# A hand-written step plan laid out anew: hedgehog linear attention plus a Mish layer on one Trainium2 core

## The chip, the cores and the metric

The kernel runs on one core of a Trainium2 chip. The metric is device time in microseconds: the median of 3 runs of the kernel before is 175.88 us (175.77 to 176.64). Engines are named as in the profile: PE is TensorE's matmul, PEld its weight loads, DVE is VectorE, ACT is ScalarE, POOL is GpSimd, SP is SyncE, which here only issues DMAs. A "q" behind an engine (SPq, ACTq) is its instruction queue.

## What is computed

The input x has 2048 rows of 512 bf16 numbers. Each row is normalised, and the result goes through two branches whose outputs are added to x.

```python
xn = _layernorm(x)                                   # 2048 x 512
qkv = xn @ wqkv                                      # 32 heads of 16
pq, pk = q @ w_phi, k @ w_phi                        # per head, 16 x 16
phi_q = concat(softmax(pq), softmax(-pq))            # 32 features a head
phi_k = concat(softmax(pk), softmax(-pk))
kv, z = phi_k^T @ v, sum of phi_k                    # over all 2048 rows
o = (phi_q @ kv) / (phi_q . z + 1e-6)
out = x + o @ wo + mish(xn @ w1 + b1) @ w2           # w1: 512 x 1792, w2: 1792 x 512
```

## The kernel before

The rows are cut into 16 tiles of 128 (numbered 0 to 15) and into four groups of four tiles. Nothing in the kernel loops: a text called `PLAN` (line 20) lists 582 steps by name, and the loop at line 710 carries them out one after the other with `step` (line 595). The order of the names is the order in which instructions stand in each engine's queue, since the tile framework's scheduler is switched off (line 158). Each engine works through its own queue in order; semaphores keep the data dependences. A last number in the names `apply`, `sums` and all that end in `=` picks the engine: 0 is ACT and 1 DVE for the steps that end in `=`; for `apply`, `sums` 0 is DVE, 1 POOL, 2 ACT.

The steps, in the order in which the work needs them:

- Normalising: `spread`, `mean` or `gather` (DVE statistics of a tile), `total` and `scatter` (the same on ACT for tile 3), `deviate` (ACT square root), `invert` (DVE reciprocal), `apply` (writes the normalised tile). Tiles 0 to 3 are then turned on PE (`flip`, line 255, four transposes into a PSUM bank) and copied to SBUF (`flip=`); tiles 4 to 15 are turned by DMA on SP's queue (`turned`, line 263).
- Weights: `foldk` multiplies the key weights with w_phi on PE (line 172, four small matmuls a step, four steps), `foldk=` casts the result into `wkv` on ACT; `fold` and `fold=` do it later for the queries. The two halves of the turned key weights `wT` come by DMA (line 167).
- Attention, keys: `first_i_kt` (tile i of the first group, a quarter of its contraction, line 632) and `logits_g_i` (four matmuls, line 662) give pk; `logits=` copies it out of PSUM, `plane` subtracts the extremes (DVE), `exp` is the exponential on ACT, `sums` and `normal` finish the softmax, `value` and `value=` give v, and `add` (line 445) adds a tile to kv on PE.
- Attention, queries: the same with s = 4 to 7 (`logits`, `logits=`, `minus=`, `shift`, `exp`, `sums`, `weigh`), then `kv` (masks kv on DVE), `turn` (DMA transpose on SP, line 418), `attend` (eight matmuls on PE into a single buffer `pnd`, line 484), `divide` (DVE), `out` (DMA transpose on SP, line 512).
- Dense branch: `unit_g_f` (four matmuls, line 288) and `unit=` (Mish on ACT, line 300), 56 of each.
- End of a tile: `second_t_0`, `second_t_1` (seven matmuls each, line 520), `project_t` (four matmuls, line 530), `residual_t` (DVE adds x, line 539), `store_t` (DMA to HBM on SP's queue, line 544; tile 15 is stored in two halves, one of them from ACT's queue).

Exponentials and Mish need different tables on ACT, so every change from `exp` to `unit=` or back costs a table load. Six PSUM banks go round in a ring (`bank`, line 130): a step on PE that opens a bank waits until the step that empties the bank opened six before it has run. `warm` is a matmul of ones that nobody reads (line 582): eleven run at the start (line 588), two more stand in the plan.

Of the kernel before, what the change touches and what calls it, by code (L numbers as in the profile page):

```python
# [26 lines left out]
logits=_0_3_1 root_1 logits=_0_2_1 first_1_3 value=_1_0 value_2 logits=_0_1_1 unit_0_6 bias=  # L27
apply_6_0 unit_0_2 apply_7_0 unit=_0_6 plane_0_0 turned_6 apply_4_2 value_0 apply_5_2 unit_0_11
value=_0_0 turned_4 unit_0_12 value=_2_0 unit=_0_2 unit_0_4 spread_11 unit=_0_12 spread_12 unit_0_3
unit=_0_11 plane_0_1 unit=_0_4 unit_0_10 unit=_0_3 value_3 w2 unit=_0_10 logits_1_2 spread_9  # L30
logits_1_3 exp_0_1 value=_3_1 value_4 spread_13 logits=_1_3_0 sums_0_1_1 spread_10 logits_1_1
exp_0_0 spread_8 value_7 value=_4_0 gather_2 logits=_1_1_0 logits=_1_2_1 unit_0_0 exp_0_3 spread_14
logits_1_0 root_2 spread_15 exp_0_2 unit_0_8 sums_0_0_0 value=_7_0 unit_1_13 gather_3 apply_8_0
unit_1_9 apply_11_0 apply_9_0 unit=_0_0 apply_10_0 unit_0_1 logits=_1_0_1 unit=_1_9 root_3 turned_10
unit_1_3 sums_0_2_0 unit=_0_8 unit=_1_13 turned_8 unit_1_11 normal_0_0 unit=_0_1 unit_1_6 apply_12_2
apply_15_2 value_6 unit=_1_3 unit_0_5 apply_14_0 wo unit=_1_11 plane_1_0 add_0_0 unit=_1_6 unit_1_12
turned_14 value=_6_0 unit_1_5 apply_13_2 unit_1_2 unit=_1_12 turned_12 unit=_0_5 sums_0_3_0 unit_1_7
unit=_1_2 unit_1_1 plane_1_1 unit=_1_7 unit=_1_5 logits_2_3 unit=_1_1 value_5 logits=_2_3_0
logits_2_0 normal_0_1 logits_3_3 exp_1_3 add_0_1 logits_2_1 exp_1_0 logits_2_2 sums_1_3_0 value=_5_0
sums_1_0_1 exp_1_1 unit_2_3 logits=_2_0_1 add_0_2 logits=_2_1_0 sums_1_1_0 add_0_3 logits_3_2  # L40
logits=_3_3_0 exp_1_2 unit_2_2 normal_1_0 masks logits=_2_2_0 unit_2_1 logits_3_0 unit=_2_3 unit_1_8
sums_1_2_0 logits=_3_2_0 wq unit_1_0 unit=_2_2 unit=_2_1 plane_2_0 unit_3_1 unit=_1_0 unit_1_4
logits=_3_0_0 unit=_1_8 unit_2_9 unit=_3_1 unit_3_12 normal_1_1 add_1_1 unit=_3_12 unit_3_9
unit=_2_9 logits_3_1 unit=_1_4 plane_2_1 add_1_0 logits=_3_1_0 unit_1_10 unit=_3_9 add_1_3
unit=_1_10 fold_1 fold_2 add_1_2 fold=_1_0 unit_2_11 fold=_2_0 fold_0 plane_3_0 unit=_2_11 unit_3_13
fold=_0_0 unit_2_8 unit=_3_13 value_14 unit=_2_8 value_9 plane_3_1 value_13 exp_2_2 value_8
value=_9_0 value_11 value=_14_0 exp_2_3 value=_13_1 sums_2_2_1 value_12 value=_8_1 exp_2_1 value_15
value=_11_1 value=_12_1 exp_2_0 fold_3 value_10 value=_15_1 exp_3_2 sums_2_1_1 sums_2_3_0 unit_0_13
exp_3_3 unit_2_5 fold=_3_1 value=_10_1 unit_3_10 exp_3_0 normal_2_1 unit_0_7 exp_3_1 unit_3_11
unit_3_8 sums_2_0_0 sums_3_1_1 unit=_0_13 add_2_3 add_2_2 unit=_2_5 unit_3_2 normal_2_0 unit=_3_10  # L50
unit_3_5 unit=_3_11 unit=_0_7 logits_4_2 unit=_3_2 unit_3_7 unit=_3_8 sums_3_0_0 sums_3_3_1
logits_4_3 unit=_3_7 unit=_3_5 add_2_0 sums_3_2_0 add_2_1 unit_2_4 logits=_4_2_0 normal_3_0
logits_4_0 minus=_4_2_0 logits=_4_3_0 logits_4_1 logits=_4_0_0 minus=_4_3_0 unit_2_0 logits=_4_1_0
shift_4_1 unit_2_13 unit=_2_4 minus=_4_0_0 unit_0_9 unit=_2_13 minus=_4_1_0 unit_3_3 unit=_2_0
unit_3_4 unit=_3_3 shift_4_0 unit=_0_9 unit_2_6 unit=_3_4 add_3_1 logits_5_1 unit=_2_6 logits_5_3
# [4 lines left out]
turn_0_1 unit=_3_6 logits_6_0 minus=_5_2_0 logits=_6_1_0 logits_7_1 turn_0_0 kv unit=_2_12  # L60
logits_7_0 logits=_6_3_0 turn_1_0 shift_5_0 minus=_6_1_0 logits_7_3 minus=_6_3_0 logits=_6_0_0
second_0_0 turn_1_1 second_2_0 shift_5_1 exp_5_0 exp_5_1 second_0_1 minus=_6_0_0 logits=_7_1_0
attend_0_0 second_1_0 sums_5_1_1 minus=_7_1_0 divide_0_0 logits=_7_3_0 logits=_7_0_0 sums_5_0_0
out_0_0 attend_0_1 minus=_7_3_0 second_2_1 minus=_7_0_0 divide_0_1 exp_5_2 second_3_0 weigh_2
second_1_1 shift_6_0 turn_2_0 out_0_1 logits_7_2 attend_1_0 second_4_0 turn_2_1 divide_1_0 exp_6_0
sums_5_2_0 project_0 exp_6_1 out_1_0 sums_6_0_1 attend_1_1 logits=_7_2_0 residual_0 second_3_1
exp_5_3 divide_1_1 minus=_7_2_0 project_1 out_1_1 shift_6_1 second_5_0 store_0 attend_2_0 second_5_1
divide_2_0 exp_6_3 project_2 sums_6_1_0 exp_6_2 out_2_0 sums_6_3_1 attend_2_1 second_4_1 divide_2_1
residual_2 out_2_1 project_3 residual_1 sums_6_2_1 second_6_0 residual_3 store_2 sums_5_3_0
second_7_0 weigh_3 second_8_0 weigh_4 turn_3_0 project_4 turn_3_1 shift_7_0 second_7_1 turn_4_0  # L70
second_10_0 turn_4_1 weigh_5 exp_7_1 project_5 store_3 exp_7_0 attend_3_0 second_10_1 divide_3_0
sums_7_0_1 residual_4 out_3_0 attend_3_1 second_6_1 divide_3_1 turn_5_0 sums_7_1_0 attend_4_0
second_8_1 turn_5_1 divide_4_0 second_12_0 weigh_6 out_3_1 out_4_0 project_6 residual_5 shift_7_1
attend_4_1 turn_6_0 second_12_1 store_1 second_9_0 divide_4_1 exp_7_3 project_7 residual_6 exp_7_2
out_4_1 sums_7_3_1 attend_5_0 second_9_1 divide_5_0 residual_7 out_5_0 attend_5_1 project_8
divide_5_1 turn_6_1 second_13_0 sums_7_2_0 store_5 second_11_0 weigh_7 out_5_1 project_9 turn_7_0
attend_6_0 second_11_1 divide_6_0 turn_7_1 attend_6_1 out_6_0 project_10 divide_6_1 second_13_1
store_4 residual_8 residual_10 store_8 project_11 out_6_1 attend_7_0 second_14_0 divide_7_0
residual_11 out_7_0 attend_7_1 project_12 divide_7_1 second_15_0 residual_12 out_7_1 residual_9
# [6 lines left out]
def kernel(  # L86
# [43 lines left out]
    def bank(name, dtype=FP32):  # L130
        return ps.tile([P, 512], dtype, name=name, tag="mm")
# [22 lines left out]
    block = consts.tile([P, 8, 16], BF16, name="block")  # L154
# [423 lines left out]
    dve, act = nc.vector.tensor_copy, nc.scalar.copy  # L578

    warm = bank("warm")  # L580

    def keep_warm():
        nc.tensor.matmul(  # L583
            warm[:].rearrange("p (k c) -> p k c", k=4), lhsT=ones[:],
            rhs=ones[:, None, :].to_broadcast([P, 4, P]), start=True, stop=True,
        )

    for _ in range(11):
        keep_warm()

    kvp = ExitStack()
# [150 lines left out]
```

## Time and profile before

| | |
|---|---|
| median of 3 runs | 175.88 us |
| the profiled execution, whole time | 175.89 us |
| its span, first to last instruction | 174.1 us |
| PE busy | 169.0 us, 1040 matmuls |
| DVE busy | 151.9 us, 268 instructions |
| ACT busy | 112.0 us, 167 instructions |
| POOL busy | 49.1 us, 91 instructions |
| read from HBM, written | 6.84 MB, 2.10 MB |

The span and the whole time differ by 1.8 us that lie around the program. In the profile a line such as L290 is a line of the kernel; "128x512" is partitions by elements. A timeline or chain row begins with the start in microseconds from the span's start, then its length. A row of a chain of waits merges neighbouring pieces of the same kind. A busy time of a matmul contains the filling of the pipeline: one of 512 columns is booked with 379 ns, while four in a row take 0.86 us, as the chain shows.

### The profile page before, as it was taken

What the parts mean: (1) busy time and instruction counts of PE and PEld (TensorE: products, weight loads), DVE (VectorE), ACT (ScalarE), POOL (GpSimd) and SP (SyncE); (2) the same over time, 40 slices, a digit from 0 to 9 for tenths busy, and PEclk for the clock granted to TensorE, in tenths of its full rate; (3) what the DMA queues carried; (4) which work ended last, traced back from release to release, by engine and by line L of the source; (5) the groups of instructions that cost most, each with busy time, mean ns of one, the idle gap of its engine ahead of it and who ended that gap; (6) DMA issues with size and microseconds to landing.
All of it is one profiled execution on the core that took longest, in us unless ns stands there. A gap on an engine that the chain in (4) does not pass through costs nothing.

```text
span 174.1 us, 2834 instructions
## 1 busy us (share of the span) xinstructions
PE 169.0 (97%) x1040; PEld 83.3 (48%) x1040; DVE 151.9 (87%) x268; ACT 112.0 (64%) x167; POOL 49.1 (28%) x91
## 2 busy tenths in 40 slices
PE   7999999999999999999999999999999999999991
PEld 2644444444544644455445444445544544545660
DVE  2999999999899999999899997999999999966722
ACT  4938999999997999998989999535400402100000
POOL 6021048100660008594008204115560410500000
PEclk9999999999999999999999999999999999999999
DMA  5999992878000000000000191163226677376571
GB/s 152 270 365 378 112 336 84 133 187 168 0 0 0 4 0 0 2 0 4 0 0 0 32 184 30 30 145 73 57 60 138 144 169 124 63 177 162 68 230 62
DMA packets 45226, 18.03 MB, mean 104 GB/s; under 512 B 37148, under 2 KB 45212, under 8 KB 45212
## 3 DMA queue, kind: packets, MB, share of 16 engines
q1 hardware_dynamic: 44524, 17.26, 43.2%
q10 hardware_dynamic: 688, 0.59, 1.1%
q8 instruction: 8, 0.13, 0.3%
q14 instruction: 6, 0.05, 0.1%
HBM read 6.84 MB, written 2.10 MB: 51 GB/s over the span
## 4 chain that ended last, share of the span: by engine, by line
PE 88%; ACT 4%; DVE 4%; issue 1%; DVEq 0%; ACTq 0%
PE po L525 28%; PE ph L290 23%; PE pproj L275 21%; PE po L534 7%; PE warm L583 3%; PE pnd L489 2%; ACT e L378 2%; PE pkv L452 2%; DVE m L341 2%; DVE e L348 1%; PE pfold L175 1%; ACT L378 1%; PE ptr L258 1%; DVE x_sb L542 1%; ACT acts L300 0%
## 5 line engine op out<-in xcount | busy, mean ns | idle before, releaser
L290 PE MATMUL ph<-xnT,w_sb 128*128 128x512 bf16 x224 | 51.8, 379 | 0.2 <-ACT acts L300 0.2
L525 PE MATMUL po<-w_sb,acts 128*128 128x512 bf16 (+1 forms) x238 | 51.8, 366 | 0.0
L378 ACT ACTIVATE e<-e 128x1024 bf16<-128x1024 bf16 x28 | 28.1, 1053 | 27.7 <-DVE e L348 27.7
L392 POOL TENSOR_TENSOR t<-e 128x512 f32<-128x512 bf16 x13 | 16.9, 1300 | 78.8 <-ACT e L378 78.8
L300 ACT ACTIVATE acts<-ph,b1f 128x512 bf16<-128x512 f32 x56 | 35.2, 702 | 1.6 <-PE ph L290 1.6
L290 PEld LDWEIGHTS <-w_sb 128*128 128x128 bf16 x224 | 21.5, 98 | 25.2 <-issue 0.5
L525 PEld LDWEIGHTS <-acts 128*128 128x128 bf16 x238 | 22.4, 98 | 22.3
L275 PE MATMUL pproj<-wkv,xnT 128*128 128x512 bf16 x128 | 29.8, 379 | 0.0
L275 PEld LDWEIGHTS <-xnT 128*128 128x128 bf16 x192 | 18.3, 98 | 21.2 <-issue 0.2
L388 DVE TENSOR_REDUCE sums<-e 128x64 f32<-128x1024 bf16 x15 | 18.0, 1210 | 0.6 <-ACT e L378 0.6
L392 POOL TENSOR_TENSOR t<-t 128x256 f32<-128x256 f32 (+1 forms) x28 | 15.8, 565 | 2.2
L534 PE MATMUL po<-wqk,ob 128*128 128x512 bf16 (+1 forms) x68 | 16.3, 366 | 0.0
L275 PE MATMUL pproj<-wqk,xnT 128*128 128x512 bf16 x64 | 15.1, 379 | 0.0
L542 DVE TENSOR_TENSOR x_sb<-po,x_sb 128x512 bf16<-128x512 f32 (+1 forms) x17 | 10.7, 652 | 4.3 <-PE po L534 4.2
L198 DVE BATCH_NORM_STATS2 stats<-x_sb 128x6 f32<-128x512 bf16 x15 | 9.7, 682 | 2.4 <-DMA x_sb<-in_A_x_dram 2.3
L505 DVE TENSOR_TENSOR ob<-pnd,r 128x512 bf16<-128x512 f32 x16 | 11.1, 692 | 0.6
L439 DVE TENSOR_TENSOR e<-e,r 128x2048 bf16<-128x2048 bf16 x8 | 9.8, 1228 | 0.3
L504 DVE RECIPROCAL r<-pnd 128x32 f32<-128x32 f32 x16 | 5.7, 354 | 4.7 <-PE pnd L489 4.4
L534 PEld LDWEIGHTS <-ob 128*128 128x128 bf16 x68 | 6.4, 98 | 6.5
L489 PEld LDWEIGHTS <-qT 128*128 128x128 bf16 x128 | 6.2, 97 | 3.8 <-issue 1.5
L434 DVE RECIPROCAL r<-sums 128x128 bf16<-128x128 f32 x8 | 7.6, 946 | 0.4 <-POOL sums L392 0.3
L348 DVE TENSOR_TENSOR e<-e,m 128x2048 bf16<-128x2048 bf16 x6 | 7.4, 1225 | 0.3
(81 smaller groups left out, 185.7 us busy)
## 6 DMA issues: line engine op xcount, KB each, us to landing
out_dram<-x_sb SPq DMA_DIRECT2D x15, 128.0 KB, 1.8
w_sb<-in_B_w_dram SPq DMA_DIRECT2D x2, 896.0 KB, 7.9
x_sb<-in_A_x_dram SPq DMA_DIRECT2D x3, 512.0 KB, 9.8
w_sb<-in_B_w_dram SPq DMA_DIRECT2D x2, 640.0 KB, 6.3
wkv<-in_A_wqkv_dram SPq DMA_DIRECT2D x1, 512.0 KB, 4.9
w_sb<-in_B_w_dram SPq DMA_DIRECT2D x1, 512.0 KB, 7.0
wqk<-in_A_wo_dram SPq DMA_DIRECT2D x1, 512.0 KB, 4.6
x_sb<-in_A_x_dram ACTq DMA_DIRECT2D x1, 384.0 KB, 3.3
```

The source lines that it names most:

```text
L198: nc.vector.bn_stats(statistics(t)[0][:, t % TPG, :], x_sb[:, t, :])
L275: nc.tensor.matmul(pp, lhsT=xnT[:, t, kt, :], rhs=w[:, kt, :], start=(kt == 0), stop=(kt == KT - 1),)
L290: nc.tensor.matmul(ph[:], lhsT=w1_sb[:, kt, f * P : (f + 1) * P], rhs=xnT[:, g * TPG : (g + 1) * TPG, kt, :], start=(kt == 0), stop=(kt == ...
L300: nc.scalar.activation(acts[:, f, g * 512 : (g + 1) * 512], ph[:], ACT.Mish, bias=b1f[:, f : f + 1])
L378: nc.scalar.activation(v, v, ACT.Exp)
L388: nc.vector.reduce_sum(out, part, axis=AX.X)
L392: nc.gpsimd.tensor_tensor(out=to[:], in0=part[:, :, 0:n], in1=part[:, :, n : 2 * n], op=ALU.add)
L439: nc.vector.tensor_tensor(out=vv, in0=vv, in1=r2[:, :, None, :].to_broadcast([P, 128, 8, 2]), op=ALU.mult)
L505: nc.vector.tensor_tensor(out=o_t.rearrange("p (u v g d) -> p u v g d", u=2, v=4, g=4), in0=nd[:, :, :, 0:64].rearrange("p u v (g d) -> p ...
L525: nc.tensor.matmul(po[:, c], lhsT=acts[:, f, t * P : (t + 1) * P], rhs=w2_sb[:, f, c], start=(f == 0), stop=False,)
L534: nc.tensor.matmul(po[:, c], lhsT=oT_of[h][:, 2 + t % 2, j * P : (j + 1) * P], rhs=wo_sb[:, j, c], start=False, stop=(j == 3),)
L542: nc.vector.tensor_tensor(out=y, in0=po[:, c], in1=y, op=ALU.add)
```

## The change

The plan is replaced as a whole. It has 581 steps instead of 582: the same ones, except for one `warm` fewer and for some steps that change engine. One matmul of ones fewer also runs ahead of the plan, 10 instead of 11. All matmuls that are used are the same in number and size.

- First tiles: tile 0 is turned before any `foldk`, and tiles 0, 2, 3, 1 are normalised and turned in that order (before: 0, then 3 and 1, then 2). The first `first` steps stand between the last turns.
- Engines: `logits=` 23 on ACT and 9 on DVE become 26 and 6, `value=` 9 and 7 become 8 and 8, `sums` 18 on DVE and 14 on POOL become 17 and 15, `apply` 11 on DVE and 5 on ACT become 12 and 4, of the first turns' copies tile 0 moves from ACT to DVE and tile 1 from DVE to ACT.
- Stores: each `store` follows its `residual` by a few steps. Before the last `out` there are 11 stores on SP's queue instead of 7. Every store is issued in the order 1, 0, 2, 3, 4, ... 15.
- The end from `project_14` on (six steps) is the same in both.

```diff
 PLAN = """
-spread_0 block mean_0 deviate_0_1 invert_0_1 total_3 spread_1 foldk_0 apply_0_0 scatter_3 foldk_1
-mean_1 flip_0 warm warm spread_2 deviate_1_1 deviate_3_1 invert_1_1 foldk=_1_0 mean_2 invert_3_1 apply_3_0
-deviate_2_1 apply_1_0 foldk=_0_0 flip_3 foldk_2 invert_2_1 apply_2_0 foldk_3 flip=_0_0 flip_1
-flip=_3_1 flip_2 foldk=_2_0 first_0_0 flip=_1_1 first_3_0 foldk=_3_0 flip=_2_1 first_0_1 first_3_1
-spread_5 first_1_0 bias first_2_0 spread_7 first_1_1 first_2_1 first_0_2 spread_4 first_3_2
-first_2_2 first_1_2 spread_6 first_0_3 first_3_3 logits=_0_0_0 first_2_3 gather_1 value_1
...
-normal_3_1 logits_5_0 exp_4_1 unit_2_7 exp_4_0 unit_3_0 logits=_5_1_1 sums_4_1_1 exp_4_2
-logits=_5_0_1 unit_2_10 minus=_5_1_0 logits=_5_3_1 add_3_0 exp_4_3 add_3_3 minus=_5_3_1 add_3_2
-logits_6_2 minus=_5_0_1 sums_4_2_1 unit_3_6 sums_4_0_0 unit=_2_7 logits_5_2 sums_4_3_0 unit=_3_0
-unit_2_12 unit=_2_10 weigh_0 logits=_6_2_0 logits_6_1 logits=_5_2_0 logits_6_3 minus=_6_2_0 weigh_1
...
-second_14_1 store_6 store_7 store_10 project_13 store_12 store_9 second_15_1 residual_13 store_13
-store_11 project_14 project_15 residual_14 store_14 residual_15 store_15
+spread_0 block mean_0 deviate_0_1 invert_0_1 total_3 spread_2 apply_0_0 scatter_3 mean_2 flip_0
+spread_1 foldk_1 deviate_2_1 foldk_0 warm flip=_0_1 deviate_3_1 foldk=_0_0 invert_2_1 foldk_2 invert_3_1
+apply_2_0 foldk_3 foldk=_1_0 mean_1 flip_2 apply_3_0 first_0_0 deviate_1_1 flip=_2_1 flip_3
+foldk=_2_0 first_0_1 invert_1_1 first_2_0 apply_1_0 foldk=_3_0 first_0_2 flip=_3_1 first_2_1 flip_1
+first_3_0 flip=_1_0 first_0_3 spread_6 first_3_1 first_2_2 logits=_0_0_0 spread_7 first_1_0
+first_3_2 first_1_1 spread_5 first_2_3 bias value_1 logits=_0_2_0 spread_4 bias= first_1_2 gather_1
+value=_1_0 first_3_3 first_1_3 root_1 logits=_0_3_1 value_2 logits=_0_1_0 unit_0_6 value=_2_1
...
+minus=_4_2_0 logits_4_0 unit=_3_8 unit_3_11 logits=_4_0_0 shift_4_1 unit=_3_5 unit_3_4 minus=_4_0_0
+unit_0_9 unit=_3_4 unit=_3_11 unit_0_7 unit=_0_9 shift_4_0 logits_5_3 unit=_0_7 add_3_2 add_3_0
+logits_5_0 exp_4_2 add_3_1 logits_5_2 logits=_5_3_1 exp_4_3 sums_4_2_1 logits_5_1 logits=_5_0_1
+exp_4_1 minus=_5_3_1 unit_3_0 minus=_5_0_1 exp_4_0 unit_2_10 logits=_5_1_1 add_3_3 logits=_5_2_0
+sums_4_1_1 sums_4_0_0 unit_2_12 minus=_5_1_0 minus=_5_2_0 unit_2_7 kv logits_6_0 sums_4_3_0
+logits_6_1 unit=_3_0 unit=_2_10 weigh_0 logits_6_2 unit=_2_12 logits_6_3 logits=_6_0_0 unit=_2_7
...
+residual_4 sums_7_1_1 turn_5_0 divide_3_1 second_8_1 store_4 residual_5 attend_4_0 store_5
+second_10_1 divide_4_0 out_3_1 sums_7_0_1 attend_4_1 turn_5_1 project_6 divide_4_1 second_12_0
+out_4_0 residual_6 shift_7_1 second_9_0 store_6 out_4_1 attend_5_0 project_7 weigh_6 exp_7_2
...
+project_12 second_15_0 store_11 residual_12 store_12 project_13 second_15_1 residual_13 store_13
+project_14 project_15 residual_14 store_14 residual_15 store_15
 """
...
-    for _ in range(11):
+    for _ in range(10):
         keep_warm()
```

More of the change, by code (lines that the diff above doesn't have):

```diff
@@ L26 @@
-first_2_2 first_1_2 spread_6 first_0_3 first_3_3 logits=_0_0_0 first_2_3 gather_1 value_1
[L27 to L54, printed above, removed]
@@ L61 @@
[L61 to L78, printed above, removed]
@@ new lines @@
+unit=_0_10 unit_0_11 unit=_0_3 value_3 unit=_0_11 w2 value_6 spread_10 logits_1_2 exp_0_2 spread_11
+logits_1_3 spread_8 exp_0_0 spread_15 logits_1_0 value=_3_0 gather_2 logits_1_1 spread_14 root_2
+logits=_1_2_0 value=_6_1 exp_0_1 value_5 spread_13 exp_0_3 unit_1_7 logits=_1_1_1 apply_11_0
+unit_1_2 logits=_1_3_0 apply_10_0 value=_5_0 apply_8_0 unit_0_1 apply_9_0 logits=_1_0_0 spread_12
+sums_0_1_1 turned_8 unit_0_5 sums_0_3_0 unit_1_3 turned_10 unit=_0_1 gather_3 sums_0_0_0 unit=_1_7
+unit_1_13 unit=_1_2 root_3 unit_0_8 sums_0_2_0 unit=_0_5 unit_0_0 unit=_1_13 normal_0_0 unit=_0_8
@@ new lines @@
+unit_1_12 unit=_1_3 unit_1_6 unit=_0_0 unit=_1_12 unit_1_9 wo apply_13_0 apply_15_2 plane_1_0
+unit_2_8 unit=_1_6 unit_1_11 apply_12_2 unit=_2_8 turned_12 value_4 unit=_1_11 unit_1_1 value=_4_0
+apply_14_0 plane_1_1 turned_14 unit=_1_9 logits_2_1 unit=_1_1 value_7 logits=_2_1_0 logits_2_0
+logits_2_3 normal_0_1 exp_1_3 logits_2_2 value=_7_0 add_0_0 exp_1_0 unit_2_11 sums_1_3_0
+logits=_2_0_0 sums_1_0_1 unit_1_4 exp_1_2 logits=_2_3_1 logits_3_2 exp_1_1 sums_1_2_0 unit_2_1
+logits=_2_2_0 sums_1_1_0 add_0_2 unit_1_5 masks add_0_1 normal_1_1 logits_3_3 unit=_2_11 unit=_1_4
@@ new lines @@
+add_0_3 unit_1_0 logits=_3_2_0 unit=_2_1 unit_3_12 wq unit=_1_5 normal_1_0 add_1_2 unit=_1_0 add_1_3
+logits_3_0 unit=_3_12 logits=_3_3_0 unit_3_9 logits=_3_0_0 plane_2_0 logits_3_1 unit=_3_9 unit_2_9
+unit_1_10 unit=_2_9 logits=_3_1_0 unit_2_3 plane_2_1 unit=_1_10 unit_1_8 unit=_2_3 add_1_0 unit=_1_8
+add_1_1 fold_0 fold_2 fold=_0_0 fold_1 unit_3_13 fold=_2_0 plane_3_0 fold=_1_0 unit_2_2 unit=_3_13
+unit_3_1 unit=_2_2 value_9 unit=_3_1 value_14 plane_3_1 fold_3 value_13 exp_2_1 value_10 value=_9_0
```

29 lines of the change are left out of this document (26 added, 3 removed).

## The prediction

> **What bounds the kernel now.** I read the page first (busy times), then the chain of waits in order of time, then the waits of PE, then the timelines of ACT and SP where the chain leaves PE. Below stand one line of the page, rows of the chain (start, length), one row of PE's timeline (13.81), one of its waits (us, times, longest), and further rows of the chain.
>
> ```profile
> PE 169.0 (97%) x1040; PEld 83.3 (48%) x1040; DVE 151.9 (87%) x268; ACT 112.0 (64%) x167; POOL 49.1 (28%) x91
> 1.12 4.88 PE warm L583 x11
> 6.00 0.58 PE pfold L175 x8
> 6.57 0.22 PE ptr L258 x4
> 6.80 0.43 PE warm L583 x2
> 7.23 0.36 PE ptr L258 x4
> 7.58 0.45 PE pfold L175 x8
> 8.03 0.46 PE ptr L258 x8
> 8.49 1.17 PE pproj L275 x5
> 9.66 0.11 PE pb L635
> 9.77 4.21 PE pproj L275 x19
> 13.81 1.89 PE L290 MATMUL ph<-xnT,w_sb 128*128 128x512 bf16 x8
> ...
> PE ph L290 <- ACT acts L300: 0.2, 1, 0.2
> ...
> 107.72 0.25 PE pnd L489 x8
> ...
> 169.49 1.02 DVE x_sb L542 x2
> 170.51 0.33 DVEq L737
> ```
>
> PE sets the time. A matmul of 512 columns takes 0.215 us (0.43 / 2), from 9.77 on PE's rows follow each other at about that (4.21 / 19), and the list of its waits has one entry behind the start, of 0.2 us. So work taken off DVE, ACT, POOL or SP is worth nothing by itself; the kernel gains only where PE starts its useful work earlier, where that one wait goes, or behind PE's end. It loses wherever a new wait stands in front of a matmul. The matmuls that are used stay the same, so there is little to gain: what lies between the ones and 9.77, the one wait, and the 4.6 us from 169.49, where DVE follows PE, to the end of the span at 174.1.
>
> **1. The start.** Useful PE work begins at 6.00 by the chain. From there to 9.77 lie 16 `foldk`, 16 turns, 5 `first` and the turn of b1. At full rate that is 32 x 0.056 (0.45 / 8) + 5 x 0.215 + 0.11 = 3.0 us; the rows take 3.77. The 0.8 us between are the two ones in the plan (0.43), slower first matmuls, and short waits. What the new order can start, and when, comes from DVE and ACT:
>
> ```profile
> 5.16 0.40 DVE L250 TENSOR_SCALAR xn<-x_sb,mv,rstd 128x512 bf16<-128x512 bf16 x1
> 6.72 0.73 DVE L250 TENSOR_SCALAR xn<-x_sb,mv,rstd 128x512 bf16<-128x512 bf16 x2
> 7.95 1.10 DVE L625 COPY xnT<-ptr 128x512 bf16<-128x512 bf16 x3
> 6.02 0.47 ACT L219 ACTIVATE rstd<-mv,eps 128x1 f32<-128x1 f32 x2
> 8.23 1.09 ACT L629 CAST wkv<-pfold 128x512 bf16<-128x512 f32 x2
> L558 SPq DMA_DIRECT2D w_sb<-in_B_w_dram x2: 496/502/507, 6.0 to 6.5; - x2
> DMA to landing us min/median/max: 7.0/7.9/8.8
> ```
>
> Ten ones at 0.44 each (4.88 / 11) end near 5.5. The turn of tile 0 needs its `apply`, which ends at 5.56 (5.16 + 0.40) and does not move: PE idles 0.1 to 0.2 us. Turn 5.6 to 6.0, eight `foldk` to 6.5, one `warm` to 6.7, eight `foldk` to 7.2. DVE copies tile 0 from 6.3 to 6.6 (0.36 each, 1.10 / 3), the square roots of tiles 2 and 3 are done at 6.5 (6.02 + 0.47), two reciprocals and `apply_2` follow the copy (in before 0.23 us lay between the square roots and 6.72, and 0.37 is one `apply`) and end near 7.3, so the second turn is at 7.4 and `first_0_0` at 7.6, against 8.49 in the chain. From there ACT's casts of `wkv` gate: from 6.7 on, one each 0.5 us (1.09 / 2), with a square root between them, the third done at 8.5 and the fourth at 9.0. Taking the `first` steps as their casts and copies come ready, `first_0_3` ends at 9.6, seven `first` and all turns done. Nine more `first` (1.94), the turn of b1 (0.11), `value_1` and `value_2` (1.73) put `unit_0_6` at 13.4. In before it began at 13.81. Gain 0.4 us. Bounds: it cannot begin before its half of w1 has landed, 6.0 + 7.0 = 13.05, which caps the gain at 0.75; if the casts or the copies each slip by one 0.36 us copy, nothing is left, so 0 is the other bound. I take 0.4, the result of the walk.
>
> The eleventh matmul of ones is worth nothing by itself: it stood before `apply_0` was ready. The one in the plan is worth its 0.215 (0.43 / 2) and is within the 0.4.
>
> **2. The wait at 96.95.** `unit_2_12` waits for `unit=_2_7`, which empties its bank six openings back.
>
> ```profile
> 89.23 1.28 ACT L378 ACT_TABLE_LOAD   x1 [0.56 <-DVE e L348]
> 90.53 2.95 ACT L378 ACTIVATE e<-e 128x1024 bf16<-128x1024 bf16 x3
> 93.38 0.58 ACT L329 ACTIVATE wkv<-pproj 128x512 bf16<-128x512 f32 x1
> 93.86 1.04 ACT L378 ACTIVATE e<-e 128x1024 bf16<-128x1024 bf16 x1
> 94.92 1.28 ACT L300 ACT_TABLE_LOAD   x1
> 96.22 1.84 ACT L300 ACTIVATE acts<-ph,b1f 128x512 bf16<-128x512 f32 x3
> 95.73 1.03 PE L275 MATMUL pproj<-wqk,xnT 128*128 128x512 bf16 x4
> 96.95 1.02 PE L290 MATMUL ph<-xnT,w_sb 128*128 128x512 bf16 x4 [0.20 <-ACT acts L300]
> ```
>
> The four matmuls from 95.73 fill 0.86, so PE stood from 96.59 to 96.95: 0.36 us. ACT was late because it idled 0.56 for DVE's `shift` and then ran table, four `exp`, a copy, table. In the new plan `exp_4_2` and `exp_4_3` come first, whose `shift_4_1` stands before `shift_4_0`. Counted from the start of `unit_0_7`, with 0.86 for four matmuls and 0.25, as the eight of an `attend`, for an `add`: its `unit=` ends at 1.7, table to 3.0, four `exp` at 0.96 to 6.8, three copies at 0.5 to 8.3, table to 9.6, `unit=_3_0` to 10.2. PE comes to `logits_6_0`, which needs the last of the three copies, at 8.8, and to `logits_6_2`, which needs `unit=_3_0`, at 10.5. Margins 0.5 and 0.3: the wait goes, worth 0.36, with bounds 0 and 0.36.
>
> The plan has other such blocks (`exp_0`, `exp_1`); the same count leaves 0.2 us at `unit_0_5` and 0.35 at `unit_1_0`. Thin, but PE stood only once in 160 us of a plan of the same kind. For new short waits I take 0.1, with bounds 0 and 1.1 (three blocks at 0.36).
>
> **3. The stores.** The first row is the nine stores at the end of SP's queue, the second the last two of them alone; the page's rows give KB and us from issue to landing.
>
> ```profile
> 165.20 6.00 SPq L546 DMA_DIRECT2D out_dram<-x_sb  x9
> 170.21 0.99 SPq L546 DMA_DIRECT2D out_dram<-x_sb  x2
> L546 SPq DMA_DIRECT2D out_dram<-x_sb x16: 332/446/585, 120.8 to 170.9; - x16
> out_dram<-x_sb SPq DMA_DIRECT2D x15, 128.0 KB, 1.8
> out_dram<-x_sb SPq DMA_DIRECT2D x1, 64.0 KB, 2.4
> ```
>
> The seven that wait there need at most 7 x 0.585 = 4.1 us from 165.20, to 169.3, and `store_14` is issued at 170.21 because `residual_14` ends there. The queue is free before the last tile is ready, so issuing them earlier moves the end by 0. What follows PE's end is the same six steps: two adds on DVE, the last half's issue, its landing, the program's close. Bounds: 0 to -0.6, if the last half lands in the 1.8 of the others instead of 2.4.
>
> What the stores cost lies earlier: four more of them stand ahead of transposes on SP's queue, 4 x 0.585 = 2.3 us of issue over 60. A transpose `out` for `project` lands by this row:
>
> ```profile
> L513 SPq DMA_TRANSPOSE ob<-ob x16: 1189/1197/1875, 109.1 to 163.4; - x16
> DMA to landing us min/median/max: 2.4/2.5/4.3
> ```
>
> The shortest way from an `out` to its `project` in the new plan, counted in matmuls on PE, is `out_3_1`: two `attend` (0.25 each), `project_6` (0.86) and two `second` (7 x 0.215 each), 4.4 us. 2.5 to land and 1.2 for the two stores right ahead make 3.7. Cost 0, with up to 1.1 if it lands in 4.3 (4.3 + 1.2 - 4.4).
>
> **4. Steps that change engine.** DVE gives up three copies and one `sums`, and takes one `value=` and one `apply`; ACT and POOL move by less than 3 us. DVE is 87% busy and PE hides it, so 0; where it would come out, at `divide` between two `attend`, the plan has fewer pairs with a single `second` between them than before (3 against 6).
>
> Sum against the profiled execution's 175.89: -0.4 - 0.36 + 0.1 + 0 + 0 = 175.2. The median of the runs, 175.88, is the same to 0.01, so nothing is added.
>
> **The rivals.** *All margins hold and the start reaches its cap*: -0.75 - 0.36, 174.8; if only the start and the wait come out and no new wait, 175.1. For it: PE waited once in 160 us in a plan of the same kind. Against it: casts of `wkv` on ACT, in order, are what gates 7.6 to 9.0.
>
> *The gain is given back in new short waits*: three blocks at 0.36 plus the 0.1, about 175.9 to 176.2. For it: margins of 0.2 to 0.35.
>
> *SP's queue* (slower). A store waits for its `residual`, and every transpose behind it waits too: `store_4` and `store_5` ahead of `out_3_1`, and likewise at `out_4_1`, `out_5_1`, `out_6_1`, `out_7_1`. At the longest landing each costs 1.1 as above; it decides from the point where a store's residual ends less than 3.7 us before the `project` that the `out` behind it feeds. Two such give 175.2 + 2.2 = 177.4. Against it: transposes land in 2.5 at the median, and most stores stand 1.5 us of matmuls or more behind their `residual`.
>
> *The clock* (slower). The chain shows 11 ones in 4.88 us, 0.44 each, and two later ones in 0.43: PE ran at half rate up to some place in the first eight `foldk` (0.58 against 0.45), near 6.1, after 5.0 us without a gap. Now it idles up to 0.2 us at 5.5, and then come transposes. If the 5.0 us began again, half rate would last from 6.1 to 10.6, 4.5 us; at half rate that does 2.25 us of work instead of 3.9 (4.5 less some 0.6 of waits in the walk), a loss of 1.7, which gives 176.9. [...]
>
> **How the numbers follow.** The forecast, 175.0 to 175.6, has 0.45; the rival with no new wait and a better start (under 175.0) 0.30; short waits (to 176.3) 0.10; SP's queue 0.09; the clock 0.06. 0.5% is 0.88 us, about what a measurement of this kernel can tell from no change: faster is under 175.00, slower over 176.76. So faster 0.30, same 0.45 + 0.10 = 0.55, slower 0.15. The range 174.7 to 176.9 holds the first three, reaches to the clock's 176.9 and leaves out two stalls of the queue; the likeliest's own is 175.0 to 175.6.
>
> **What would show it.** Right: `unit_0_6` near 13.4; no wait of PE for `acts` near 96; the chain on PE from 9.6 to 169; the last store issued as long behind PE's end as now (0.75 to 1.4 us). Wrong: ones or `foldk` at half rate behind 6.5 us; PE waiting for `ob` or `qT` behind SP; several waits on `acts`; an earlier end behind the last `project`.

## The result and the profile after

The kernel after takes 174.57 us (median of 6 runs, 174.39 to 175.06), the kernel before beside it 176.33 us (6 runs, 175.77 to 176.83): a ratio of 0.990, 95% interval 0.988 to 0.993. Every ratio below is likewise the time over that of the kernel before, run beside it. Run once more later, unchanged (the run a_again below), it took 174.96 us against 176.16: 0.993 (0.992 to 0.994). So the change gains 1.2 to 1.8 us, where 0.7 was forecast against the profiled execution.

The profiled execution after takes 174.82 us, its span is 173.1 us, against 175.89 and 174.1. Three lines of its page: the span, the busy times, and the share of each engine in the chain that ended last.

```profile
span 173.1 us, 2832 instructions
PE 167.2 (97%) x1021; PEld 82.8 (48%) x1038; DVE 151.1 (87%) x266; ACT 113.1 (65%) x168; POOL 51.0 (29%) x95
PE 72%; DVE 18%; DMA 3%; SPq 3%; issue 3%; DVEq 0%
```

PE's work is as before (some matmul records are missing: the page has 1021 of them). But 18% of the chain now runs over DVE; before it was 4%:

```profile
PE 88%; ACT 4%; DVE 4%; issue 1%; DVEq 0%; ACTq 0%
```

The waits of PE after (us in all, times, longest), and rows of the chain in order of time (start, length):

```profile
PE warm L582 <- DVE ones L563: 1.1, 1, 1.1
PE ptr L258 <- DVE xn L250: 0.4, 1, 0.4
PE pproj L275 <- DMA wkv<-in_A_wqkv_dram: 0.4, 1, 0.4
...
5.55 5.80 DMA wkv<-in_A_wqkv_dram
11.35 0.05 issue
11.40 2.56 PE pproj L275 x11
13.96 0.02 issue
13.98 0.03 DVE vext L282
...
46.50 0.61 DVE p L310
47.11 0.04 issue
47.16 1.02 PE ph L290 x4
...
95.26 1.73 PE ph L290 x8
96.99 4.10 PE pproj L275 x19
...
169.34 1.02 DVE x_sb L542 x2
170.36 0.33 DVEq L736
```

Three things are to be seen. First, the wait for `acts` near 97 is gone: at 96.99 PE goes straight from one step to the next. Second, two new waits have come: the value weights land at 11.35 and PE stands for 0.4 us in front of `value_1`, and from 13.98 to 47.11 the chain runs on DVE, which ends in a copy for which `unit_2_1` waits. That wait is not in the list of waits, and shows in PE's timeline:

```profile
45.98 1.03 PE L275 MATMUL pproj<-wkv,xnT 128*128 128x512 bf16 x4
47.16 1.02 PE L290 MATMUL ph<-xnT,w_sb 128*128 128x512 bf16 x4
```

Four matmuls from 45.98 fill 0.86, to 46.84; the next start at 47.16, 0.32 later. Third, PE ends only 0.15 us earlier: `residual_14`, the row of L542, starts at 169.34 instead of 169.49. The whole is 1.07 us shorter (175.89 less 174.82), so some 0.9 lie behind PE's end. Rows of the view of the DMAs between 170.5 and 174 us show them: the packets of each queue (count, MB, share of 16 engines) and then the two halves of the last store, with KB and us to landing. By their bytes q1 carries SP's DMAs and q10 ACT's; q14 is marked as carrying instructions. Before:

```profile
q1 hardware_dynamic: 288, 0.20, 17.3%
q10 hardware_dynamic: 144, 0.07, 6.4%
q14 instruction: 1, 0.01, 1.1%
out_dram<-x_sb ACTq DMA_DIRECT2D x1, 64.0 KB
out_dram<-x_sb SPq DMA_DIRECT2D x1, 64.0 KB, 2.4
```

And after:

```profile
q1 hardware_dynamic: 288, 0.20, 17.4%
q10 hardware_dynamic: 144, 0.07, 6.5%
out_dram<-x_sb ACTq DMA_DIRECT2D x1, 64.0 KB
out_dram<-x_sb SPq DMA_DIRECT2D x1, 64.0 KB, 1.5
```

The last half of the last tile lands in 1.55 us instead of 2.44, 0.89 less, and the one other difference in the window is a packet of the instruction queue q14. The trace has its time: it is 8 KB, starts at 171.92 us and takes 628 ns, to 172.55. In before all packets of the last store but nine start by 172.06; eight packets of 512 bytes and the closing one of 4 bytes start from 172.54 on, the moment that the instruction packet is through. So it looks as if they waited for it; the trace does not name a packet's DMA engine, so where they waited is not shown. In after the packets of the last store are all started by 171.91, and the nearest packet of q14 is at 147.72.

### The profile page after: what moved, and what is told of

The parts are those of the page before. It is cut to its first block, busy times and chain, and to the rows that moved or that the text cites. A ratio compares the mean times of both kernels' runs of the same rounds, so it can differ in the third digit from the quotient of the medians.

```text
span 173.1 us, 2832 instructions
## 1 busy us (share of the span) xinstructions
PE 167.2 (97%) x1021; PEld 82.8 (48%) x1038; DVE 151.1 (87%) x266; ACT 113.1 (65%) x168; POOL 51.0 (29%) x95
## 4 chain that ended last, share of the span: by engine, by line
PE 72%; DVE 18%; DMA 3%; SPq 3%; issue 3%; DVEq 0%
PE po L525 28%; PE ph L290 17%; PE pproj L275 15%; PE po L534 7%; DMA wkv<-in_A_wqkv_dram 3%; DVE m L361 3%; DVE e L369 3%; DVE stats L198 3%; DVE xn L250 2%; PE pnd L489 2%; PE pkv L452 2%; DVE sums L388 2%; SPq L167 2%; DVE r L434 1%; DVE e L439 1%
## 5 line engine op out<-in xcount | busy, mean ns | idle before, releaser
L392 POOL TENSOR_TENSOR t<-e 128x512 f32<-128x512 bf16 x14 | 18.5, 1324 | 65.0 <-ACT e L378 65.0
L392 POOL TENSOR_TENSOR t<-t 128x256 f32<-128x256 f32 (+1 forms) x30 | 16.9, 563 | 2.4
L388 DVE TENSOR_REDUCE sums<-e 128x64 f32<-128x1024 bf16 x14 | 16.7, 1208 | 0.7 <-ACT e L378 0.7
L542 DVE TENSOR_TENSOR x_sb<-po,x_sb 128x512 bf16<-128x512 f32 (+1 forms) x17 | 10.9, 654 | 5.9 <-PE po L534 5.8
L534 PE MATMUL po<-wqk,ob 128*128 128x512 bf16 (+1 forms) x65 | 15.6, 366 | 0.2
L327 ACT CAST e<-pproj 128x512 bf16<-128x512 f32 x12 | 6.9, 602 | 2.7 <-PE pproj L275 1.3
L310 ACT CAST p<-pproj 128x512 bf16<-128x512 f32 x13 | 7.6, 595 | 0.7 <-PE pproj L275 0.7
```

The lines of the kernel that those rows point to most:

```text
L388: nc.vector.reduce_sum(out, part, axis=AX.X)
L392: nc.gpsimd.tensor_tensor(out=to[:], in0=part[:, :, 0:n], in1=part[:, :, n : 2 * n], op=ALU.add)
L534: nc.tensor.matmul(po[:, c], lhsT=oT_of[h][:, 2 + t % 2, j * P : (j + 1) * P], rhs=wo_sb[:, j, c], start=False, stop=(j == 3),)
L542: nc.vector.tensor_tensor(out=y, in0=po[:, c], in1=y, op=ALU.add)
```

## The experiments

Theory A, the author's supposition from these rows: the packet of q14 brings ACT's next instructions (the theory's "fetch"), and its place follows how many instructions ACT has got through. In before it then comes just behind ACT's part of the last store (issued at 170.54, the packet at 171.92) and in front of the last half's packets. After has three more ACT instructions (192 ahead of ACT's last store instead of 189, waits and DMA issues counted), so it would come earlier, at 147.72. Rival B: it is the early stores that empty the queue or the DMA engines. For the 0.15 at PE's end the question was what took back the rest of the 0.4 and 0.36.

Four kernels first. **b_act3**: before, with three small instructions on ACT.

```diff
-exp_7_3 project_7 residual_6 exp_7_2 out_4_1
+exp_7_3 project_7 residual_6 exp_7_2 idle idle idle out_4_1
...
+        elif kind == "idle":
+            nc.scalar.activation(root[:], eps[:], ACT.Exp)
```

> The kernel before with three added activations of 128x1 on ACT right behind its last exponential, results unused. Theory A (instruction fetch): in the trace of before an 8 KB packet of the instruction queue q14 begins at 171.9 us, between the last half-store's issue (170.9) and its landing (2.4 us, where the changed kernel's took 1.55); ACT crosses into a new block of its instructions there, and three instructions more bring that crossing to about 148 us, as in the changed kernel. Expected: no q14 packet behind 165 us, last half-store lands in 1.5 to 1.7 us, time 0.6 to 0.9 us shorter than before. Theory B (the early stores clear the DMA queue for the last one): nothing about the stores is changed, so the landing stays at 2.4 and the time within 0.2 us.

175.26 us (174.87 to 175.53), ratio 0.9948 (0.9932 to 0.9963). More work, 0.91 us less time. The same window of its trace:

```profile
q1 hardware_dynamic: 288, 0.20, 17.3%
q10 hardware_dynamic: 144, 0.07, 6.5%
out_dram<-x_sb ACTq DMA_DIRECT2D x1, 64.0 KB
out_dram<-x_sb SPq DMA_DIRECT2D x1, 64.0 KB, 1.5
```

The packet is gone from the end, and the landing is that of after. But it did not come to about 148 us, as expected: the last two packets of q14 are at 136.58 and 150.62 (in before at 150.73 and 171.92), and the trace does not say which engine a packet is for. The wait of 0.36 near 97 is still there, and PE's work from `unit_0_6` to the last issue is as long as in before (157.05 us against 157.06).

**b_stores**: before, with every store moved close behind its `residual`, in after's manner.

```diff
-second_14_1 store_6 store_7 store_10 project_13 store_12 store_9 second_15_1 residual_13 store_13
+second_14_1 store_9 project_13 second_15_1 residual_13
...
+attend_3_1 store_4
+attend_4_1 store_5
+out_4_1 store_6
+attend_5_1 store_7
```

> The kernel before with every store moved up to two steps behind its residual, nothing else changed. Theory A: ACT's queue is as before, so the q14 packet still meets the last half-store: time within 0.2 us of before, unless transposes behind the stores come late (up to 1 us slower). Theory B: the last half-store lands in 1.5 to 1.7 us and the time is 0.6 to 0.9 us shorter.

176.08 us (175.78 to 176.64), ratio 0.9995 (0.9983 to 1.0008). The packet is there and the landing is long:

```profile
q14 instruction: 1, 0.01, 1.5%
out_dram<-x_sb SPq DMA_DIRECT2D x1, 64.0 KB, 2.7
```

**a_late**: after, with the stores of tiles 6, 7, 9, 10, 11 and 12 held back to the end.

```diff
-residual_12 store_12 project_13
+residual_12 store_6 store_7 store_10 project_13 store_12 store_9
-residual_13 store_13
+residual_13 store_13 store_11
...
```

> The changed kernel with stores 6, 7, 9, 10, 11 and 12 held back to the end of SP's queue, where before had its seven. Theory A: the time stays that of the changed kernel, 1.5 to 1.9 us shorter than before (174.5), last landing 1.5 to 1.7 us. Theory B: the last half-store lands in about 2.4 us and 0.7 to 0.9 us of the gain is lost (175.3).

175.05 us (174.51 to 175.26), ratio 0.9927 (0.9909 to 0.9944); the last half lands in 1.53 us. The time is above the 174.5 of theory A, but its ratio is that of the kernel after when run again (a_again below, 0.9928). With b_stores this drops rival B: where the stores stand sets neither the landing nor the time.

**a_actless**: after, with three copies given to DVE so that ACT has fewer instructions.

```diff
-logits=_7_1_0
+logits=_7_1_1
...
-logits=_7_3_0
+logits=_7_3_1
...
-logits=_7_0_0
+logits=_7_0_1
```

> The changed kernel with the copies logits=_7_0, logits=_7_1 and logits=_7_3 on DVE instead of ACT, so that ACT's last store stands four instructions earlier in its queue, one earlier than in the kernel before. Theory A: the q14 packet is back at the end (about 171 us) or just ahead of it; if it meets the last half-store, the landing is 2.0 us or more and the time 0.5 to 0.9 us longer than the changed kernel's 174.57. Theory B: landing stays at 1.5 to 1.7 us. Both: DVE takes 2 us more, hidden by PE, up to 0.3 us.

176.40 us (175.97 to 176.89), ratio 1.0014 (1.0000 to 1.0027). The time rose, but not through the landing, which stayed at 1.54: the q14 packet was back at the end, at 173.73, yet 1.46 us behind the last issue (in after the store's last packet starts 1.19 us behind that issue). What cost the time was the edit itself, since DVE now came late to `divide`:

```profile
118.35 0.41 PE L489 MATMUL pnd<-kvm,qT 128*128 128x68 bf16 x8 [1.03 <-DVE ob L505]
```

So this run tells of the packet only that 1.46 us behind the issue it cost the landing nothing, and the reverse test was made again without new work on DVE. Beside it ran the two halves of the change alone, and one edit of the loads.

**s_start**: after's steps up to `unit_0_6` and its ten ones, then before's order. **s_rest**: the reverse. Both with the three `idle` steps of b_act3, so that the packet of q14 is out of the way (in b_act3 none is behind 150.62) and b_act3 is what they are compared with.

```diff
-spread_0 block mean_0 deviate_0_1 invert_0_1 total_3 spread_1 foldk_0 apply_0_0 scatter_3 foldk_1
+spread_0 block mean_0 deviate_0_1 invert_0_1 total_3 spread_2 apply_0_0 scatter_3 mean_2 flip_0
...
 unit_0_6 apply_6_0 unit_0_2 apply_7_0 unit=_0_6 plane_0_0 turned_6
...
```

> The new start alone: the steps up to unit_0_6 and the ten ones as in after, from there on the order of before, and three small ACT exponentials behind exp_7_2 so that the fetch of instructions stays away from the last store. Compared with the kernel before with the same three exponentials (ratio 0.9948, 175.26 us). Theory of the prediction (the start is worth 0.4 us because casts and turns gate it): 0.4 below that, 174.9, ratio 0.9925, and unit_0_6 starts 0.3 to 0.5 us earlier than in the kernel before on the same loads. Rival (the loads of the value weights and of the first half of w1 gate it, whose landing does not depend on the order of the tiles): 175.1 to 175.4, ratio 0.994 to 0.996, PE waits for wkv or w_sb in front of value_1 or unit_0_6. The wait of PE near 96.9 must still be there (0.36) and the last half must land in about 1.55 us under both.

175.15 us (174.86 to 175.48), ratio 0.9940 (0.9919 to 0.9961): 0.14 us below b_act3 by the ratios, with intervals that overlap. Its waits of PE:

```profile
PE pproj L274 <- DMA wkv<-in_A_wqkv_dram: 0.4, 1, 0.4
PE ph L289 <- ACT acts L299: 0.2, 1, 0.2
```

The second is the old one near 97, the first the new one for the value weights; `unit_0_6` starts at 14.08. That is the rival's result.

> All but the start: the steps up to unit_0_6 and the eleven ones as in before, from there on the order of after, again with three small ACT exponentials behind the last exp. Compared with the kernel before with three exponentials (ratio 0.9948, 175.26 us). If the wait near 96.9 is worth its 0.36 us and the stores nothing: 174.9, ratio 0.9928. If the early stores were worth something as well, lower than 174.7. If new short waits eat the 0.36: 175.2 or more. The last half lands in about 1.55 us under all three.

174.98 us (174.81 to 175.19), ratio 0.9931 (0.9911 to 0.9952): 0.30 us below b_act3 by the ratios, with intervals that overlap too. No wait near 97, the wait near 47 is 0.30, the last half lands in 1.54.

**a_exp3**: after, without three exponentials.

```diff
-exp_6_0
...
-exp_7_0
...
-exp_7_1
```

> The kernel after with three exponentials left out (exp_6_0, exp_7_0, exp_7_1: that part of the queries' softmax is not taken), so ACT has three instructions less and nothing on PE changes. Theory of the fetch: ACT fetches its next instructions behind its last store again, near 172 us, in the way of the last half's packets: the last half lands in 2.2 to 2.8 us instead of 1.55 and the time rises by 0.6 to 1.1 us above the kernel after, to 175.2 to 175.7 (ratio 0.994 to 0.997), although less work is done. Rival (the new order, and not the count of ACT's instructions, keeps the landing short): 1.55 us and no slower than after, ratio 0.9904. If the fetch comes just behind the landing, as in the run with three copies on DVE, the time stays that of after and the page's tail is longer by less than 0.5.

175.10 us (174.53 to 175.38), ratio 0.9930 (0.9906 to 0.9955): the case that the last sentence allowed for. The packet is back at 172.77, 1.53 us behind the last issue, and the landing is 1.54. By the trace's list of ACT's instructions, with a wait that also fell away, ACT has 188 instructions ahead of its last store, one less than before's 189; the packet starts 1.53 us behind the issue instead of 1.05.

**a_exp3i**: the same with one `idle`, which makes it 189, the count of before.

```diff
-exp_6_0
...
-exp_7_0
...
-exp_7_1
...
+idle
```

> The kernel after with exp_6_0, exp_7_0 and exp_7_1 left out (that part of the softmax is not taken) and one small exponential behind the last exp, so that ACT has as many instructions ahead of its last store as in the kernel before. Theory of the fetch: it comes back about 1.0 to 1.4 us behind the last issue, the last half lands in 2.2 to 2.8 us, and the time is 0.6 to 1.1 us above the kernel after of the same call. Rival (the new order itself keeps the landing short): 1.55 us, and the time of the kernel after.

175.67 us (175.38 to 176.27), ratio 0.9974 (0.9958 to 0.9990). Its window of the DMAs, which here begins behind ACT's issue:

```profile
q14 instruction: 1, 0.01, 1.2%
out_dram<-x_sb SPq DMA_DIRECT2D x1, 64.0 KB, 2.4
```

The packet starts at 171.39, 1.01 us behind the last issue (in before 1.05), the landing is 2.43 us (in before 2.44), and again eight data packets start only when it is through (172.04). Beside it, the kernel after, unchanged:

> The kernel after, unchanged, to stand beside the others on the same chip: ratio 0.9904 as before if the loads at the start land as early as in its first runs; 0.992 to 0.994 if the wait for wkv is as long (1.0 us) as in the later traces. The last half lands in 1.55 us.

174.96 us (174.61 to 175.08), ratio 0.9928 (0.9917 to 0.9940). So a_exp3i, with less work and all of after's order in place, is 0.71 us slower than after by the medians, 0.8 by the ratios. Against a_exp3, from which it differs by the one small instruction alone, it is 0.57 slower by the medians and 0.8 by the ratios, with intervals that do not meet.

**b_exp2**: before without two exponentials, 187 ACT instructions ahead of the last store.

```diff
-exp_7_1
...
-exp_7_0
```

> The kernel before with two exponentials left out (exp_7_0 and exp_7_1: half of tile 7's part of the queries' softmax is not taken), so ACT has two instructions less ahead of its last store and PE's work is the same. Theory of the fetch, as the runs so far refine it: the fetch follows ACT's count of instructions, and two fewer move it later, behind the landing of the last half, as in the kernel after with three exponentials left out, where it came 1.5 us behind the last issue and the last half landed in 1.54. So: landing 1.55 us, time 0.8 to 0.9 us below before, ratio 0.994 to 0.996, the same as three exponentials more gave (0.9948). Rival (three exponentials more helped in some other way, by keeping ACT busy or warm before its store): fewer exponentials give 2.4 us and ratio 1.0.

176.20 us (175.81 to 176.98), ratio 1.0005 (0.9993 to 1.0016). The landing is as expected, 1.53 us with the packet at 174.62, but the time is a miss: DVE's steps moved against each other and `attend` waited.

```profile
138.95 0.42 PE L488 MATMUL pnd<-kvm,qT 128*128 128x68 bf16 x8 [0.66 <-DVE ob L504]
```

The excess over the matmuls' own time is 0.82 us there, which puts the last issue 0.90 later than in before and takes the whole 0.91 of the landing.

The runs that bear on the landing, in one table. "Packet behind issue" is the start of the last q14 packet less the last half's issue, both from the trace.

| run | ACT instructions ahead of its last store | packet behind issue, us | last half lands in, us |
|---|---|---|---|
| before | 189 | 1.05 | 2.44 |
| b_stores | 189 | 1.02 | 2.75 |
| a_exp3i | 189 | 1.01 | 2.43 |
| a_actless | 188 | 1.46 | 1.54 |
| a_exp3 | 188 | 1.53 | 1.54 |
| b_exp2 | 187 | 2.85 | 1.53 |
| after, b_act3, a_late, a_again, s_start, s_rest, and a_best, a_47, a_47w below | 192 to 194 | none behind 152 us | 1.53 to 1.55 |

Four runs aimed at the start and the wait near 47. **a_wv**: after, with the value weights loaded ahead of tiles 4 to 7, and one `idle` for the count.

```diff
+    nc.sync.dma_start(wv, wqkv_v[:, :, 2 * D : 3 * D])
     nc.sync.dma_start(x_sb[:, 4:8, :], x_v[:, 4:8, :])
     nc.sync.dma_start(b1b[:], b1_v[:, :])
-    nc.sync.dma_start(wv, wqkv_v[:, :, 2 * D : 3 * D])
```

> The kernel after with the load of the value weights issued ahead of the load of tiles 4 to 7, and one small ACT exponential behind the last exp to keep ACT's count. If the landing of wkv is what ate the start's gain, the wait in front of value_1 goes and value_1 starts near 11.0; unit_0_6 then starts when the first half of w1 lands (13.1 to 14.1 in the traces so far) or at 13.4, whichever is later: 0 to 0.4 below after, ratio 0.988 to 0.9904. Rival (something else holds value_1, or the statistics of tiles 4 to 7, now later, hold the first logits): no change or up to 0.5 slower.

175.23 us (174.66 to 176.04), ratio 0.9947 (0.9929 to 0.9965): a miss as a kernel, with the widest spread of all. Its trace, of a run of 174.76, shows the mechanism half right. PE goes through to `value_1` and `unit_0_6` starts at 13.53, but then it waits near 47 for 0.51 instead of 0.32:

```profile
11.04 0.18 PE L634 MATMUL pb<-ident,b1b 14*128 14x14 bf16 x1
11.15 2.55 PE L275 MATMUL pproj<-wkv,xnT 128*128 128x512 bf16 x11
13.53 1.24 PE L290 MATMUL ph<-xnT,w_sb 128*128 128x512 bf16 x5
...
47.10 1.02 PE L290 MATMUL ph<-xnT,w_sb 128*128 128x512 bf16 x4 [0.35 <-DVE p L310]
```

**a_best** adds to that a first piece of w1 cut to the blocks used first, and the late copy ahead of the `sums` in front of it on DVE.

```diff
-    for c in (slice(0, F // 2), slice(F // 2, F)):
+    for c in (slice(256, F // 2), slice(F // 2, F), slice(0, 256)):
...
-unit_2_11 sums_1_3_0 logits=_2_0_0 sums_1_0_1 unit_1_4 exp_1_2 logits=_2_3_1
+unit_2_11 logits=_2_3_1 sums_1_3_0 logits=_2_0_0 sums_1_0_1 unit_1_4 exp_1_2
```

> The kernel after with three edits: the value weights are loaded ahead of tiles 4 to 7; w1 is loaded in three pieces, blocks 2 to 6 first (the first three units use 6, 2, 4), then 7 to 13, then 0 and 1; logits=_2_3_1 stands ahead of sums_1_3_0 on DVE; one small exponential keeps ACT's count. If the landings of wkv and w1 gate the start and the copy gates the wait near 47: value_1 begins near 11.1 without a wait, unit_0_6 at 12.9 to 13.4, no wait near 47 (0.3 to 0.5 us in the traces of after's order), together 0.5 to 0.9 below the kernel after of the same call: ratio 0.986 to 0.989. Rival (the spread of the loads' landings sets the start whatever their order): no faster than after.

175.26 us (174.82 to 175.84), ratio 0.9942 (0.9929 to 0.9955), so no faster than after beside it (0.9928, 0.9917 to 0.9940). The wait near 47 is gone, but two others stand in its place, and the bias's load, now third, is one:

```profile
PE pproj L275 <- DVE vext L282: 0.6, 1, 0.6
PE pb L634 <- DMA b1b<-in_B_b_dram: 0.5, 1, 0.5
```

**a_47** is after with the copy moved alone; **a_47w** also loads b1, the value weights and tiles 4 to 7 in this order.

```diff
-unit_2_11 sums_1_3_0 logits=_2_0_0 sums_1_0_1 unit_1_4 exp_1_2 logits=_2_3_1
+unit_2_11 logits=_2_3_1 sums_1_3_0 logits=_2_0_0 sums_1_0_1 unit_1_4 exp_1_2
...
+    nc.sync.dma_start(b1b[:], b1_v[:, :])
+    nc.sync.dma_start(wv, wqkv_v[:, :, 2 * D : 3 * D])
     nc.sync.dma_start(x_sb[:, 4:8, :], x_v[:, 4:8, :])
-    nc.sync.dma_start(b1b[:], b1_v[:, :])
-    nc.sync.dma_start(wv, wqkv_v[:, :, 2 * D : 3 * D])
```

The load lines are a_47w's alone; it also has one `idle` behind the last exponential.

> The kernel after with one step moved: logits=_2_3_1 ahead of sums_1_3_0 on DVE, nothing else. If the wait of 0.3 us near 47 (unit_2_1 behind the bank that this copy empties) is what took back the gain of the wait at 96.9, it goes and the time is 0.3 below the kernel after: ratio 0.9905 against the 0.9928 of the kernel after in its last runs. Rival (the wait turns up at the next bank, or the later sums hold an add): no change, 0.9925 to 0.994.

174.71 us (174.42 to 175.11), ratio 0.9921 (0.9908 to 0.9933). The wait is gone, PE's matmuls follow each other there:

```profile
45.83 1.03 PE L275 MATMUL pproj<-wkv,xnT 128*128 128x512 bf16 x4
46.69 1.03 PE L290 MATMUL ph<-xnT,w_sb 128*128 128x512 bf16 x4
```

Of the 0.3, 0.14 comes back as an excess ahead of the matmul at 50.19. Against the 0.9928 (0.9917 to 0.9940) of the kernel after, the gain can't be told from none.

> The same, and the loads in the order b1, value weights, tiles 4 to 7 (after has tiles 4 to 7, b1, value weights). If the landing of wkv is what eats the start's gain and the bias's own landing what cost 0.5 in the run with wkv first: no wait in front of the bias's turn or of value_1, unit_0_6 starts at 13.3 to 13.6 instead of 13.8 to 14.1, and the time is 0.2 to 0.4 below the kernel with the copy moved alone: ratio 0.987 to 0.9895. Rival (tiles 4 to 7, now later, hold DVE and through it a value's bank near 26, as in the run with three pieces of w1): no faster than the copy alone.

174.85 us (174.72 to 175.04), ratio 0.9928 (0.9915 to 0.9941): its rival's result. `unit_0_6` starts at 13.52 with no wait ahead of it, and the time that this wins is lost at 26 us, behind DVE:

```profile
26.15 1.02 PE L275 MATMUL pproj<-wkv,xnT 128*128 128x512 bf16 x4 [0.38 <-DVE vext L282]
```

No version here beats the kernel after by more than the runs can tell.

## Why the prediction was wrong

The time fell just below the range, and the gain was about twice the forecast; run again, the kernel after took 174.96, which lies inside the range. The rival in which the start reaches its cap named 174.8, close to the measured time, but by way of the start, which gave 0.03; that its number is near is luck. What came was the last sign of being wrong that the prediction names, "an earlier end behind the last `project`". By the prediction's own parts:

**3. The stores: the term that failed.** The forecast put the end behind PE at 0, with "Bounds: 0 to -0.6, if the last half lands in the 1.8 of the others instead of 2.4". That the early stores themselves are worth nothing was right (b_stores, ratio 0.9995), and so was their cost of 0 to the transposes: no run of after's order shows PE waiting for `ob` or `qT` behind SP (the one wait for `ob`, in a_actless, is behind DVE). But the 2.4 was taken as the landing of such a store, when it was a disturbed one. The change has three instructions more on ACT ahead of its last store, which took the disturbance away from the end, and the landing went to 1.55, below even the bound; 0.89 of the 1.07 us by which the profiled execution shrank is this. The row of 15 stores at 1.8 and one of half the size at 2.4 stood in the prediction: a smaller store that lands later than larger ones asked for a cause.

The page marks the packets of q14 and q8 as instruction packets, beside the kernel's data: 8 packets of 16 KB on q8 and 6 of 8 KB on q14 in before and in after alike. At the end of before one of them came with a landing 0.89 us longer, and moving it away gained 0.91 us in b_act3.

**2. The wait at 96.95.** Right in place and size: it is gone in every trace of after's order and stands at 0.36 in the traces of before's. Of "new short waits I take 0.1, with bounds 0 and 1.1" the size was off: one came, near 47, of 0.18 to 0.51 in eight traces of after's order there (0.32 in after). The prediction looked for it behind ACT's blocks of `exp`; it is behind DVE, on which the chain runs from 14 to 47 us: `logits=_2_3`, a copy that moved from ACT to DVE, stands there behind a `sums`. The net of both is in the traces: from `unit_0_6` to the last issue PE and what follows take 157.06 us in before and 156.94 in after, 0.12 less, and 156.78 in a_47.

**1. The start.** Taken at 0.4, within bounds of 0 and 0.75; it came to 0.03 in the profiled execution (13.78 against 13.81). The walk ended with "Nine more `first` (1.94), the turn of b1 (0.11), `value_1` and `value_2` (1.73)" and set nothing for the landing of the weights that `value_1` reads, though before's page had it: issued at 5.57, 4.9 us to landing, 10.45. By that row they would still have been in time; what was missing was the spread. In the new plan three of the nine `first` stand behind `value_1`, so the walk's 13.4 has it start at 11.0 (11 matmuls, 2.4 us, earlier). PE was there in time, with the turn of b1 begun at 10.86 and done 0.11 later; the load landed at 11.35, and at 10.7 to 11.9 in the other traces with this order of loads.

```profile
10.86 0.18 PE L634 MATMUL pb<-ident,b1b 14*128 14x14 bf16 x1
11.40 2.55 PE L275 MATMUL pproj<-wkv,xnT 128*128 128x512 bf16 x11 [0.36 <-DMA wkv<-in_A_wqkv_dram]
13.78 2.54 PE L290 MATMUL ph<-xnT,w_sb 128*128 128x512 bf16 x11
```

The half of w1 that `unit_0_6` needs is the second load of this kind. The prediction took before's 13.05 as the earliest start; in after it landed at 13.61, and at 13.36 to 14.14 in the other traces with this order of loads, where `unit_0_6` starts 0.04 to 0.35 us behind it. So even without the wait for the value weights the walk's 13.4 wasn't to be had in the profiled execution. Over the traces with this order of loads `unit_0_6` starts at 13.57 to 14.31 in after's start and at 13.71 to 14.16 in before's, so the start is worth nothing that shows. Where the loads were early (a_wv and a_47w: 13.53 and 13.52) the gain came out, and DVE took it back at 26 or 47 us. "The kernel gains only where PE starts its useful work earlier" was too simple for this plan, in which DVE is busy for 32.3 of the 33 us from 14 to 47.

**4. Engine changes.** Taken at 0 because PE hides DVE. The `divide` steps did hold, but not `logits=_2_3_1` behind a `sums` near 47; a_47 shows that its place in DVE's queue makes the wait (0.32 in after, none in a_47). Whether it would be gone with the copy back on ACT wasn't tried.

**The rivals.** No stall on SP's queue came. The half rate of the start (0.44 us for a matmul of ones in before, 0.215 later) did not come again: PE idled for 0.4 us ahead of the first turn, then ran its four transposes, and the timeline of PE has the `foldk` behind them at full rate:

```profile
5.62 0.40 PE L258 MATMUL ptr<-ident,xn 128*128 128x128 bf16 x4 [0.38 <-DVE xn L250]
5.86 0.61 PE L175 MATMUL pfold<-Wbd,wT 128*128 128x128 bf16 x8
6.30 0.38 PE L582 MATMUL warm<-ones 128*128 128x512 bf16 x1
```

Eight of them fill the 0.44 from 5.86 to 6.30, 0.055 each. So the loss worked out there did not come. That the 5.0 us would begin again was the author's supposition; no run shows it. The forecast's price for new short waits was a little low in its own terms: 175.2 and three blocks at 0.36 make 176.3, as its paragraph on the numbers has it, and not 176.2.

**What stays open.** The medians of after lie 0.29 us (a_again) and 0.85 us (its first runs) further below before than the 0.91 us of b_act3, while the traces give the order of the steps 0.12 and the start about 0. The first runs of after and a_again differ by 0.39 us themselves, and how early the loads land moves the start by 0.7 between traces of one order. Where the 0.2 to 0.7 left over come from, one profiled execution of each kernel can't tell.

## What to carry to other kernels

Look at what lands last, and ask why it takes longer than its like: a tail of one or two microseconds behind the last engine is a term of its own, and it can hold a delay that no instruction of the kernel shows (here 0.89 us). A change that only adds or removes instructions on an idle engine can move the time by half a per cent (b_act3: 0.91 us of 176); before a gain is put down to an order, give the old order the same count. And when a wait is taken away from PE, count next the engine that is second in the chain: here a_wv, a_best and a_47w, which took the wait for the value weights away, gave back most of what that won, or more, within 36 us, behind DVE.

## What was not expected of the hardware

- Packets that the page marks as instruction run beside the kernel's data: 8 KB on q14, 309 to 1591 ns each within the spans of before and after, and 16 KB on q8, 876 to 2476 ns. Where one started 1.01 to 1.05 us behind the issue of the last 64 KB store (before, b_stores, a_exp3i), the store landed in 2.43 to 2.75 us, 0.9 to 1.2 more than the 1.53 to 1.55 without one. Where one started 1.46 us or more behind it (a_actless, a_exp3, b_exp2), the landing was 1.53 to 1.54.
- Near the end the place of such a packet moved with ACT's instruction count: 189, 188 and 187 instructions on ACT ahead of its last store came with a packet 1.0, 1.5 and 2.85 us behind the last issue. In the runs with 192 to 194 none is behind 152 us: the last two packets of q14 are at 136.58 and 150.62 us in b_act3, at 145.07 and 147.72 in after. Which of them is ACT's the trace doesn't say, so that the fetch comes at a fixed count (theory A) is not shown, only that the count moves it.
- The value weights, 512 KB issued at 5.5 to 6.0 us, landed between 10.45 and 11.88 us in traces with the same order of loads, and the first half of w1, issued at 5.9 to 6.4, between 13.05 and 14.14. A start that hangs on them can't be forecast closer than that.
